# Second LayerNorm transposed by DMA, a third slot for the pair sums, and a new plan for the order on TensorE

## Chip, cores, metric

One core of a Trainium2 chip. The metric is the device time of one execution in microseconds; medians of several runs, compared within the same rounds on the same chip. The kernel before was timed anew with each of the four sets of runs: medians 1119.2 to 1120.4, so times from different sets compare to about 1 us.

## The reference

A transformer block over 2048 tokens of width 1024: LayerNorm, attention with 32 heads of 32, residual, LayerNorm, a feed-forward part of width 3584 with tanh-GELU, residual. Inputs and output are bf16.

```
h  = x + softmax(q k^T * 32**-0.5) v @ wo        # q, k, v from layernorm(x) @ wqkv
h2 = h + gelu(layernorm(h) @ w1 + b1) @ w2 + b2
```

## The kernel before

The kernel first lists all its work as tasks, each with an engine, an assumed duration and its dependencies. A list scheduler then plays these tasks through on assumed clocks and writes down the order on each engine. That order is fixed in the program, and on the chip an engine stands where its next instruction still lacks an input: ScalarE stood 18.6 us ahead of the exps in the kernel before, 10.5 of them for scores. So a constant such as the assumed length of an exp changes nothing that is computed, but it changes the order.

```
def schedule(self, pick_pe, switch=0.1, ...):     # assumed cost of a change of array mode on TensorE
    ...
                    if e == E.PE:
                        if state["mode"] != t.mode:
                            start += switch
MM = 0.2140                                       # assumed: 512 columns
def c_act(n, ap_bias=False):                      # assumed: ScalarE; 0.943 us for an exp of 1024
    return 0.090 + (0.093 if ap_bias else 0.0) + n / 1200.0
...
NPS = 2                                           # slots for pair sums
NFI = 2                                           # buffers of the finish
```

Attention runs in 512 rounds (64 jobs of eight). A round is eight score matmuls (row tiles: the array is split by rows, and four heads run at once: eight matmuls of 273 ns each lie within 0.40 us in the prediction's timeline), two exps on ScalarE, one pair sum on VectorE (it adds the two halves of the exps, for the row sums of the softmax), eight value matmuls and four row-sum matmuls (column tiles: the array is split by columns). Six PSUM banks hold scores, three slots of which a round uses two; the other banks serve a job's output and one or two groups of background work.

```
for q in range(2):
    act(... a.activation(PT[:, s, 2*q:2*q+2, :], psum[:, 2*u:2*u+2, :], ACT.Exp, ...), 1024, kind="exp")
z = unit["ps"] % NPS
dve(... v.tensor_tensor(PS[:, z, :, :], PT[:, s, :, 0:256], PT[:, s, :, 256:512], ALU.add), ...)
```

The background work is projections, the output projection, FFN1 (full array) and FFN2 (column tiles). Tokens go in eight chunks of 256. At the turn of a chunk the second LayerNorm makes two tiles, one after the other through one buffer, and transposes them for FFN1:

```
def ln2_tile(R, c, t, evac):
    o, bo = R.xb.next()                           # one buffer for both tiles
    layer_norm([(hch[:, c % 2, t, :], ..., o, bo)], LN2_PRIO)
    if evac == "dma":
        dma_t(hnT[:, t, :, :], o, [bo], [B_hnT[t]], prio=-1)
    else:                                         # eight TensorE transposes and a VectorE copy
        transposes(group(f"t{c}.{t}"), o, bo, hnT[:, t, :, :], B_hnT[t], evac)
...
PLAN = [F2[0], 2, F2[1], 5, F2[2], 5, F2[3], 2]   # FFN2 groups of the older chunk, FFN1 blocks between
for c in range(2, NC):
    if c > 2:
        wo(R1, c - 1)
    ln2(R1, c - 1, "dve")
    mixed(R1, c - 1, c - 2, PLAN)
    attention(c)
```

The softmax here doesn't subtract the row's maximum and nothing guards it: scores larger than these inputs give would overflow.

Of the kernel before, what the change touches and what calls it, by code (L numbers as in the profile page):

```python
# [7 lines left out]
ACT = mybir.ActivationFunctionType  # L8
ALU = mybir.AluOpType
# [3 lines left out]
P = 128  # L13
BF = dt.bfloat16
F32 = dt.float32
# [48 lines left out]
class Graph:  # L64
# [44 lines left out]
        return t  # L109


    def schedule(self, pick_pe, switch=0.1, dma_rate=260.0, dma_lat=2.0, fetch=4.7):
        for i, t in enumerate(self.tasks):
            t.left = len(t.deps)
            for d in t.deps:
# [10 lines left out]
        n = 0  # L126
# [11 lines left out]
        while n < total:  # L138
# [5 lines left out]
            for e in self.ENGS:  # L144
                while free[e] <= now + 1e-9:
# [6 lines left out]
                    if e == E.PE:  # L152
                        t = pick_pe(rd, now, state, up)
                    else:
                        t = min(rd, key=lambda x: (x.prio, num[x]))
                        if up and t.prio > 0:

                            for (rt, _, u) in up[:6]:
                                if u.prio < t.prio and rt < now + 0.6 * t.occ:
                                    t = None  # L160
# [5 lines left out]
                    if e == E.PE:  # L166
# [3 lines left out]
                        i = state["pe"] // 256  # L170
# [142 lines left out]
def build_kernel(nc, A_x, A_wqkv, A_wo, B_w1, B_b1, B_w2, B_b2, out):  # L313
# [9 lines left out]
    SCALE = DH ** -0.5  # L323
# [25 lines left out]
    def sb(area, name, shape, dtype, split=1, parts=1):  # L349
        off, n = area.take(shape, dtype)  # L350
        h = nc.alloc_sbuf_tensor_at(name, shape, dtype, offset=off)
        step = n // split
        bufs = []
        for i in range(split):
            ps = [gr.buf("SB", off + i * step, off + (i + 1) * step, (name, i)) for _ in range(parts)]
            bufs.append(ps if parts > 1 else ps[0])
        return h, (bufs if split > 1 else bufs[0])

    top = Area(BASE)
# [25 lines left out]
    NPT = 7  # L385
    PT, B_PT_ = sb(top, "PT", [P, NPT, 4, 512], BF, 2 * NPT)
    B_PT = [B_PT_[2 * s:2 * s + 2] for s in range(NPT)]
    NPS = 2
    PS, B_PS = sb(top, "PS", [P, NPS, 4, 256], BF, NPS)
    NFI = 2  # L390
    OS, B_OS = sb(top, "OS", [P, NFI, 256], F32, NFI)
    DT, B_DT = sb(top, "DT", [P, NFI, 256], F32, NFI)
    RT, B_RT = DT, B_DT
    RB, B_RB = sb(top, "RB", [P, NFI, 8], F32, NFI)
    pt_hi = top.cur
    junk = PT[:, NPT - 1, 0:2, :]
    B_junk = B_PT[NPT - 1][0]
    NOT = 2
    F2 = [(0, 0), (0, 1), (1, 0), (1, 1)]
    OT, B_OT_ = sb(top, "OT", [P, NOT, G, 256], BF, NOT * G)  # L400
# [30 lines left out]
    R1 = Set()  # L431
# [20 lines left out]
    psum = nc.alloc_psum_tensor("ps", [P, 8, 512], F32)  # L452
# [3 lines left out]
    qd = nc.dram_tensor("q_scratch", [G, 3, P, 512], BF, kind="Internal").ap()  # L456
    B_qd = [[gr.buf() for _ in range(3)] for _ in range(G)]

    MM = 0.2140

    def c_dve_ps(n):
        return (120 + n) / 960.0 + 0.02

    def c_dve(n, x=1):
        return (62 + n / x) / 960.0 + 0.02

    def c_act(n, ap_bias=False):
        return 0.090 + (0.093 if ap_bias else 0.0) + n / 1200.0

    def pe(fns, occ, reads=(), writes=(), kind="bg", mode="full", prio=0, after=()):  # L470
        return gr.add(E.PE, fns, occ, 0.16, reads, writes, prio, kind, mode, after)
# [15 lines left out]
    def mm(g, lhsT, rhs, start, stop, reads, cols=(0, 512)):  # L487
        c0, c1 = cols
        occ = MM * (c1 - c0) / 512.0 + 0.0015
        fns = []  # L490
# [13 lines left out]
    def act(fn, n, reads=(), writes=(), prio=0, ap_bias=False, kind=""):  # L504
        return gr.add(E.Activation, fn, c_act(n, ap_bias), 0.14, reads, writes, prio, kind)

    def dve(fn, occ, reads=(), writes=(), prio=0, after=()):
        return gr.add(E.DVE, fn, occ, 0.08, reads, writes, prio, after=after)
# [157 lines left out]
    class Job:  # L666
# [10 lines left out]
        def round(self):  # L677
            r, g = self.r, self.g
            self.r += 1
            us = []  # L680
            for _ in range(2):
                us.append(unit["n"] % unit["of"])
                unit["n"] += 1
            s = unit["pt"] % NPT
            unit["pt"] += 1
            fns = []
            for i in range(2):
                for hh in range(4):
                    r0 = 32 * hh
                    fns.append(lambda p, i=i, hh=hh, r0=r0: p.matmul(  # L690
                        psum[:, 2 * us[hh // 2] + hh % 2, 256 * i:256 * i + 256],
                        KT[r0:r0 + 32, g, 256 * r + P * i:256 * r + P * i + P], QT[r0:r0 + 32, self.slot, :],
                        start=True, stop=True, tile_position=(r0, 0)))
            pe(fns, 0.217, reads=[B_KT[g][r], B_QT[self.slot]], writes=[B_ps[2 * u + k] for u in us for k in range(2)],
               kind="qk", mode="row")
            for q in range(2):
                u = us[q]
                act(lambda a, u=u, q=q: a.activation(PT[:, s, 2 * q:2 * q + 2, :], psum[:, 2 * u:2 * u + 2, :], ACT.Exp, bias=0.0, scale=SCALE),  # L698
                    1024, reads=[B_ps[2 * u], B_ps[2 * u + 1]], writes=[B_PT[s][q]], kind="exp")
            direct = self.direct or (self.final and r == 7)  # L700
            if not direct:
                z = unit["ps"] % NPS
                unit["ps"] += 1
                dve(lambda v: v.tensor_tensor(PS[:, z, :, :], PT[:, s, :, 0:256], PT[:, s, :, 256:512], ALU.add), c_dve(1024, 2),  # L704
                    reads=B_PT[s], writes=[B_PS[z]], prio=-1)
            fns = []
            for i in range(2):
                for hh in range(4):
                    fns.append(lambda p, i=i, hh=hh: p.matmul(  # L709
                        psum[32 * hh:32 * hh + 32, self.bank, 0:256], V[:, g, 2 * r + i, 32 * hh:32 * hh + 32],  # L710
                        PT[:, s, hh, 256 * i:256 * i + 256], start=r == 0 and i == 0, stop=r == 7 and i == 1,
                        tile_position=(0, 32 * hh), skip_group_check=True))
            t = pe(fns, 0.217, reads=B_PT[s] + [B_V[g][r]], writes=[self.buf], kind="pv", mode="col")
            pvs.append(t)
            job_of[t] = self
            self.dens.append((r, s if direct else z, direct))
            if len(self.dens) == 2:
                self.den(*self.dens.pop(0))
            if r == 7:
                self.den(*self.dens.pop(0))  # L720
                self.finish()
# [11 lines left out]
        def finish(self):  # L733
            g, c = self.g, self.c
            f = unit["fi"] % NFI
            unit["fi"] += 1
            dve(lambda v: v.transpose(DT[:, f, :], psum[:, self.bank, 256:512]), c_dve_ps(256),  # L737
                reads=[self.buf], writes=[B_DT[f]], prio=-1)
            if not self.final:
                dve(lambda v: v.tensor_copy(OS[:, f, :], psum[:, self.bank, 0:256]), c_dve_ps(256),  # L740
                    reads=[self.buf], writes=[B_OS[f]], prio=-1)
            dve(lambda v: v.reciprocal(RB[:, f, :], DT[:, f, :].rearrange("p (b j) -> p b j", j=32)[:, :, 0]), 0.15,
                reads=[B_DT[f]], writes=[B_RB[f]])
            dve(lambda v: v.transpose(RT[:, f, :], RB[:, f, :].unsqueeze(2).broadcast_to((P, 8, 32))), c_dve(256),
                reads=[B_RB[f]], writes=[B_RT[f]])
            dve(lambda v: v.tensor_tensor(OT[:, c % NOT, g, :], psum[:, self.bank, 0:256] if self.final else OS[:, f, :], RT[:, f, :], ALU.mult),
                c_dve_ps(256), reads=[self.buf if self.final else B_OS[f], B_RT[f]], writes=[B_OT[c % NOT][g]])

    def wblock(R, src_ap):
# [27 lines left out]
    def wo(R, c):  # L777
        for j in range(2):
            ws = wo_w(R, j)
            for t in range(2):  # L780
                wo_group(R, c, j, t, ws)

    def ln2_tile(R, c, t, evac):
        o, bo = R.xb.next()
        layer_norm([(hch[:, c % 2, t, :], B_hch[c % 2][2 * t:2 * t + 2], o, bo)], LN2_PRIO)
        if evac == "dma":
            dma_t(hnT[:, t, :, :], o, [bo], [B_hnT[t]], prio=-1)
        else:
            transposes(group(f"t{c}.{t}"), o, bo, hnT[:, t, :, :], B_hnT[t], evac)

    def ln2(R, c, evac):
        for t in range(2):
            ln2_tile(R, c, t, evac)
# [70 lines left out]
    def mixed(R, c1, c2, plan):  # L864
        blk = 0
        for p in plan:
            if isinstance(p, int):
                ffn1(R, c1, range(blk, blk + p))
                blk += p
            else:  # L870
                ffn2(R, c2, *p)
# [89 lines left out]

    b1_on_partitions()
    wo(R1, 0)
    ln2(R1, 0, "dve")
    for h in range(3):
        for g in range(G):
            spill_q(g, h)
# [3 lines left out]
    def attention(c):  # L971
        for g in range(G):
            attend(g, c)
            c2, g2 = divmod(G * c + g + NQ, G)
            if c2 < NC:
                load_q(g2, c2)
# [4 lines left out]
    for c in range(2, NC):  # L981
        if c > 2:
            wo(R1, c - 1)
        ln2(R1, c - 1, "dve")
        mixed(R1, c - 1, c - 2, PLAN)
        attention(c)
    L = NC - 1
# [195 lines left out]
```

## Time and profile before

| | before |
|---|---|
| time, median of 4 | 1120.39 us |
| first exp starts, last exp ends | 15.9, 1052.4 us |
| after the last exp | 65.6 us |
| TensorE, ScalarE busy | 96%, 93% |
| changes of array mode on TensorE | 1213 |

Most lines are in the prediction. Two more of the page: the chain of work that ended last, by engine, and the exps' group (busy time and mean length; idle time before them).

```profile
PE 81%; ACT 11%; DVE 6%; issue 1%; POOL 0%; DVEq 0%; POOLq 0%
...
L698 ACT ACTIVATE PT<-ps 128x1024 bf16<-128x1024 f32 x1024 | 966.6, 1034 | 18.6 <-PE ps L690 10.5
```

The chain that sets the end runs over TensorE for 81% of the time. ScalarE shows little idle time, but the exps' busy time of 966.6 us is longer than they need (1024 x 0.9125 = 934 us by their starts), so some 33 us of it, by these two numbers, is waiting inside records.

### The profile page before, as it was taken

The page shows a single profiled execution, that of the slowest core. Times are in us where ns is not written, and L with a number is a line of the kernel's source. Part 1 is how long each engine was busy: PE and PEld are TensorE (multiplying, and loading weights), DVE is VectorE, ACT ScalarE, POOL GpSimd, SP SyncE. Part 2 cuts the span into 40 slices and gives each one's busy share as a digit, 9 for nine tenths or more (in the row PEclk, how much of TensorE's full clock was granted, in tenths as well). Part 3 has the DMA queues.
Part 4 walks back from the last instruction along what each step waited for, and adds up shares of the span by engine and source line. Part 5 has one row for each costly group of instructions (what it writes and reads, how often), then busy time and mean ns, then how long its engine had stood idle before and what let it go on. Part 6 is the DMA issues. An engine that isn't in the chain of part 4 may idle for free.

```text
span 1118.0 us, 44121 instructions
## 1 busy us (share of the span) xinstructions
PE 1072.1 (96%) x20225; PEld 594.9 (53%) x20229; DVE 825.6 (74%) x1475; ACT 1042.5 (93%) x1135; POOL 19.2 (2%) x37
## 2 busy tenths in 40 slices
PE   8999999999999989999999999999989999999999
PEld 6646464644445635554554555456535544564485
DVE  7465756676767987887788788868878776787663
ACT  5889999999999999999999999999999999999661
POOL 1000000000000000000000000000000000000000
PEclk9999999999999999999999999999999999999999
DMA  6960100012236526484747548455837368697570
GB/s 191 197 162 4 40 4 3 4 55 87 83 97 174 165 73 204 122 258 141 217 143 225 176 126 251 134 176 162 259 95 230 97 199 244 212 264 225 165 244 20
DMA packets 248390, 165.66 MB, mean 148 GB/s; under 512 B 35979, under 2 KB 246027, under 8 KB 248204
## 3 DMA queue, kind: packets, MB, share of 16 engines
q1 hardware_dynamic: 248204, 162.83, 49.8%
q8 instruction: 159, 2.61, 1.0%
q14 instruction: 27, 0.22, 0.1%
HBM read 152.31 MB, written 7.34 MB: 143 GB/s over the span
## 4 chain that ended last, share of the span: by engine, by line
PE 81%; ACT 11%; DVE 6%; issue 1%; POOL 0%; DVEq 0%; POOLq 0%
PE ps L497 31%; PE ps L500 23%; PE ps L690 12%; ACT PT L698 11%; PE ps L709 9%; PE ps L728 5%; DVE PS L704 2%; PE ps L888 1%; DVE gT L814 1%; PE ps L580 1%; DVE stg L593 0%; DVE a_os L859 0%; DVE gT L833 0%; ACT a_th L832 0%; DVE a_sq L830 0%
## 5 line engine op out<-in xcount | busy, mean ns | idle before, releaser
L698 ACT ACTIVATE PT<-ps 128x1024 bf16<-128x1024 f32 x1024 | 966.6, 1034 | 18.6 <-PE ps L690 10.5
L704 DVE TENSOR_TENSOR PS<-PT 128x1024 bf16<-128x1024 bf16 x495 | 328.1, 683 | 78.5 <-PE ps L728 42.5
L500 PE MATMUL ps<-hnT,w1r 128*128 128x256 bf16 x1632 | 206.7, 273 | 8.0 <-DVE gT L814 5.6
L690 PE MATMUL ps<-QT,KT 32*128 32x256 bf16 x4096 | 204.0, 273 | 9.3 <-ACT PT L698 8.2
L497 PE MATMUL ps<-w2r,gT 128*32 128x512 bf16 x3056 | 210.3, 382 | 1.4 <-DVE gT L833 1.2
L709 PE MATMUL ps<-PT,V 128*32 128x256 bf16 x4096 | 184.9, 274 | 6.0 <-ACT PT L698 4.6
L500 PEld LDWEIGHTS ps<-hnT,w1r 128*128 128x128 bf16 x1632 | 146.9, 98 | 60.7 <-issue 38.2
L690 PEld LDWEIGHTS ps<-QT,KT 32*128 32x128 bf16 x4096 | 60.8, 92 | 162.3 <-ACT PT L698 99.4
L728 PE MATMUL ps<-PS,ones 128*32 128x256 bf16 x1980 | 139.0, 276 | 2.2 <-DVE PS L704 1.7
L497 PE MATMUL ps<-xnT,Wall 128*32 128x512 bf16 x1888 | 128.2, 381 | 4.3 <-DVE stg L593 2.8
L709 PEld LDWEIGHTS ps<-PT,V 128*32 128x32 bf16 x4096 | 96.4, 96 | 58.4 <-issue 17.3
L497 PEld LDWEIGHTS ps<-w2r,gT 128*32 128x32 bf16 x3056 | 71.6, 96 | 67.2 <-issue 25.1
L814 DVE TENSOR_TENSOR gT<-ps,b1f 128x512 bf16<-128x512 f32 x98 | 67.3, 687 | 32.5 <-PE ps L500 31.4
L728 PEld LDWEIGHTS ps<-PS,ones 128*32 128x32 bf16 x1980 | 51.4, 95 | 42.9 <-DVE PS L704 22.6
L833 DVE SCALAR_TENSOR_TENSOR gT<-a_th,gT 128x1024 bf16<-128x1024 f32 x49 | 59.7, 1219 | 14.6 <-ACT a_th L832 14.4
L497 PEld LDWEIGHTS ps<-xnT,Wall 128*32 128x32 bf16 x1888 | 44.2, 96 | 46.8 <-issue 13.2
L497 PE MATMUL ps<-w1r,OT 128*32 128x512 bf16 x896 | 61.4, 381 | 2.0 <-DVE hch L774 1.4
L830 DVE SCALAR_TENSOR_TENSOR a_sq<-a_sq,gT 128x1024 bf16<-128x1024 bf16 x49 | 59.8, 1221 | 0.9
L497 PE MATMUL ps<-Wall,xnT 128*32 128x256 bf16 x1536 | 52.4, 274 | 1.8 <-DVE V L593 0.9
L832 ACT ACTIVATE a_th<-a_sq 128x1024 f32<-128x1024 bf16 x49 | 51.8, 1058 | 0.2
L737 DVE STREAM_TRANSPOSE DT<-ps 128x256 f32<-128x256 f32 x64 | 28.6, 446 | 24.5 <-PE ps L728 24.5
L497 PEld LDWEIGHTS ps<-Wall,xnT 128*32 128x32 bf16 x1536 | 37.9, 96 | 11.4 <-issue 7.7
(86 smaller groups left out, 630.5 us busy)
## 6 DMA issues: line engine op xcount, KB each, us to landing
w2r<-in_B_w_dram SPq DMA_DIRECT2D x105, 512.0 KB, 5.7
w1r<-in_B_w_dram SPq DMA_DIRECT2D x102, 512.0 KB, 4.7
w1r<-in_A_wo_dram SPq DMA_DIRECT2D x28, 512.0 KB, 4.1
wk<-in_B_w_dram SPq DMA_DIRECT2D x9, 512.0 KB, 6.1
xrb<-in_A_x_dram SPq DMA_DIRECT2D x16, 256.0 KB, 4.2
Wall<-in_A_wqkv_dram SPq DMA_DIRECT2D x16, 256.0 KB, 5.3
wv<-in_B_w_dram SPq DMA_DIRECT2D x8, 512.0 KB, 7.7
a_x<-in_A_x_dram SPq DMA_DIRECT2D x28, 128.0 KB, 3.9
```

Of the source, the lines that this page charges most:

```text
L497: fns.append(lambda p, j=j: p.matmul(dst(32 * j, 32 * j + 32), lhsT[:, 32 * j:32 * j + 32], rhs, start=start, stop=stop, tile_position=(0, ...
L500: t.alt = [lambda p: p.matmul(dst(0, P), lhsT, rhs, start=start, stop=stop, skip_group_check=True)]
L690: fns.append(lambda p, i=i, hh=hh, r0=r0: p.matmul(psum[:, 2 * us[hh // 2] + hh % 2, 256 * i:256 * i + 256], KT[r0:r0 + 32, g, 256 * r + P ...
L698: act(lambda a, u=u, q=q: a.activation(PT[:, s, 2 * q:2 * q + 2, :], psum[:, 2 * u:2 * u + 2, :], ACT.Exp, bias=0.0, scale=SCALE), 1024, r ...
L704: dve(lambda v: v.tensor_tensor(PS[:, z, :, :], PT[:, s, :, 0:256], PT[:, s, :, 256:512], ALU.add), c_dve(1024, 2), reads=B_PT[s], writes= ...
L709: fns.append(lambda p, i=i, hh=hh: p.matmul(psum[32 * hh:32 * hh + 32, self.bank, 0:256], V[:, g, 2 * r + i, 32 * hh:32 * hh + 32], PT[:, ...
L728: fns.append(lambda p, i=i, hh=hh, src=src: p.matmul(psum[32 * hh:32 * hh + 32, self.bank, 256:512], ones32[:, :], src[:, hh, :], start=False,
L737: dve(lambda v: v.transpose(DT[:, f, :], psum[:, self.bank, 256:512]), c_dve_ps(256), reads=[self.buf], writes=[B_DT[f]], prio=-1)
L814: gate[c] = dve(lambda v, xh=xh, fc=fc, grp=grp: v.tensor_tensor(xh, psum[:, grp.bank, :].rearrange("p (f n) -> p f n", f=2), b1f[:, fc:fc ...
L830: dve(lambda v: v.scalar_tensor_tensor(v4(sq), v4(sq), C2, xh, ALU.add, ALU.mult), c_dve(n), reads=[b_sq] + b_xh, writes=[b_sq], prio=1)
L832: act(lambda a: a.activation(th, sq, ACT.Tanh, bias=0.0, scale=K2 / 2), n, reads=[b_sq], writes=[b_th], prio=-1, kind="tanh")
L833: t = dve(lambda v: v.scalar_tensor_tensor(xh, v4(th), 1.0, xh, ALU.add, ALU.mult), c_dve(n), reads=[b_th] + b_xh, writes=b_xh, prio=1)
```

## The change

Its intent: take the second LayerNorm's transposes off TensorE and VectorE, use one finish buffer instead of two so that a third pair-sum slot fits, and plan the order with constants nearer to the chip. Call the parts D (transposes by DMA), S (slot), P (planner's constants).

The diff is cut to its main lines:

```diff
-    def schedule(self, pick_pe, switch=0.1, dma_rate=260.0, dma_lat=2.0, fetch=4.7):
+    def schedule(self, pick_pe, switch=0.108, dma_rate=260.0, dma_lat=2.0, fetch=4.7):
-    NPS = 2
+    NPS = 3
-    NFI = 2
+    NFI = 1
     ... (OS, DT, RB become separate tensors, indexed [f][:] instead of [:, f, :])
-    MM = 0.2140
+    MM = 0.2150
-        return 0.090 + (0.093 if ap_bias else 0.0) + n / 1200.0
+        return 0.072 + (0.093 if ap_bias else 0.0) + n / 1200.0
+    EXP = (0.930, 0.915)
-                act(lambda a, u=u, q=q: ... ACT.Exp ..., kind="exp")
+                t = act(lambda a, u=u, q=q: ... ACT.Exp ..., kind="exp")
+                t.occ = EXP[q]
-    ln2(R1, 0, "dve")
+    ln2(R1, 0, "dma")
-        ln2(R1, c - 1, "dve")
+        ln2(R1, c - 1, "dma")
```

More of the change, by code (lines that the diff above doesn't have):

```diff
@@ L387, in build_kernel @@
     B_PT = [B_PT_[2 * s:2 * s + 2] for s in range(NPT)]
-    NPS = 2
+    NPS = 3
     PS, B_PS = sb(top, "PS", [P, NPS, 4, 256], BF, NPS)
-    NFI = 2
-    OS, B_OS = sb(top, "OS", [P, NFI, 256], F32, NFI)
-    DT, B_DT = sb(top, "DT", [P, NFI, 256], F32, NFI)
+    NFI = 1
+    OS, DT, RB, B_OS, B_DT, B_RB = [], [], [], [], [], []
+    for i in range(NFI):
+        for h, b, nm, n in ((OS, B_OS, "OS", 256), (DT, B_DT, "DT", 256), (RB, B_RB, "RB", 8)):
+            x, y = sb(top, f"{nm}{i}", [P, n], F32)
+            h.append(x)
+            b.append(y)
     RT, B_RT = DT, B_DT
-    RB, B_RB = sb(top, "RB", [P, NFI, 8], F32, NFI)
     pt_hi = top.cur
@@ L697, in round @@
                 u = us[q]
-                act(lambda a, u=u, q=q: a.activation(PT[:, s, 2 * q:2 * q + 2, :], psum[:, 2 * u:2 * u + 2, :], ACT.Exp, bias=0.0, scale=SCALE),
+                t = act(lambda a, u=u, q=q: a.activation(PT[:, s, 2 * q:2 * q + 2, :], psum[:, 2 * u:2 * u + 2, :], ACT.Exp, bias=0.0, scale=SCALE),
                     1024, reads=[B_ps[2 * u], B_ps[2 * u + 1]], writes=[B_PT[s][q]], kind="exp")
+                t.occ = EXP[q]
             direct = self.direct or (self.final and r == 7)
@@ L736, in finish @@
             unit["fi"] += 1
-            dve(lambda v: v.transpose(DT[:, f, :], psum[:, self.bank, 256:512]), c_dve_ps(256),
+            dve(lambda v: v.transpose(DT[f][:], psum[:, self.bank, 256:512]), c_dve_ps(256),
                 reads=[self.buf], writes=[B_DT[f]], prio=-1)
             if not self.final:
-                dve(lambda v: v.tensor_copy(OS[:, f, :], psum[:, self.bank, 0:256]), c_dve_ps(256),
+                dve(lambda v: v.tensor_copy(OS[f][:], psum[:, self.bank, 0:256]), c_dve_ps(256),
                     reads=[self.buf], writes=[B_OS[f]], prio=-1)
-            dve(lambda v: v.reciprocal(RB[:, f, :], DT[:, f, :].rearrange("p (b j) -> p b j", j=32)[:, :, 0]), 0.15,
+            dve(lambda v: v.reciprocal(RB[f][:], DT[f][:].rearrange("p (b j) -> p b j", j=32)[:, :, 0]), 0.15,
                 reads=[B_DT[f]], writes=[B_RB[f]])
-            dve(lambda v: v.transpose(RT[:, f, :], RB[:, f, :].unsqueeze(2).broadcast_to((P, 8, 32))), c_dve(256),
+            dve(lambda v: v.transpose(RT[f][:], RB[f][:].unsqueeze(2).broadcast_to((P, 8, 32))), c_dve(256),
                 reads=[B_RB[f]], writes=[B_RT[f]])
-            dve(lambda v: v.tensor_tensor(OT[:, c % NOT, g, :], psum[:, self.bank, 0:256] if self.final else OS[:, f, :], RT[:, f, :], ALU.mult),
+            dve(lambda v: v.tensor_tensor(OT[:, c % NOT, g, :], psum[:, self.bank, 0:256] if self.final else OS[f][:], RT[f][:], ALU.mult),
                 c_dve_ps(256), reads=[self.buf if self.final else B_OS[f], B_RT[f]], writes=[B_OT[c % NOT][g]])
```

## The prediction

> **What bounds the kernel now.** I read first the page's busy line and the slices, then the costliest groups, then busy time by stretches of 20 us, then the waits, then single stretches of the timeline. The busy line:
>
> ```profile
> PE 1072.1 (96%) x20225; PEld 594.9 (53%) x20229; DVE 825.6 (74%) x1475; ACT 1042.5 (93%) x1135; POOL 19.2 (2%) x37
> ```
>
> Two engines are nearly full, TensorE and ScalarE, and VectorE has room. Busy records stretch where work overlaps or waits, so I went to starts in the trace. Exps (line L698) that follow one another without a wait start 0.904 and 0.921 us apart in turn, mean 0.9125. There are 1024 of them, so 934 us; the other ScalarE work between the first exp (15.9 us) and the end of the last (1052.4 us) is 49 tanh at 0.93 us and 12 us of copies in the lead: together 992 us in a stage of 1036.5 us. TensorE's work in the same stage is close to that too. Its cost per piece is the distance from start to start: 0.217 us for four column tiles of 512 columns, 0.110 for 256 columns, 0.056 for a transpose, and about 0.104 us more wherever the array changes between row tiles (scores), column tiles (most of the rest) and the full array (FFN1 and transposes). In the timeline this last cost looks so:
>
> ```profile
> 153.63 0.83 PE L497 MATMUL ps<-Wall,xnT 128*32 128x256 bf16 x24
> ...
> 154.40 0.40 PE L690 MATMUL ps<-QT,KT 32*128 32x256 bf16 x8
> ...
> 154.72 0.51 PE L497 MATMUL ps<-Wall,xnT 128*32 128x256 bf16 x12
> ```
>
> The columns are start, length, engine, line and count. The 24 are six packs of four, 6 x 0.110 = 0.66, yet scores start 0.77 after them: 0.11 for the change. The eight scores are two packs, 0.22, and the next work starts 0.32 after them: 0.10 again. The instruction order of this kernel has 1213 such changes, so 126 us of TensorE's time. With these costs the whole TensorE program adds up to 1053 us: 11 before the first score, 977 between the first and last score, 65 after the last.
>
> So between first and last exp ScalarE has 992 us of work and TensorE 977 us, in 1036 us. Neither is the only bound: scores can run ahead by little more than one exp (three score buffers, two used per round), so a round with too much TensorE work makes ScalarE wait, and one with too little leaves TensorE waiting. The stretches show both cases and the tail:
>
> ```profile
> 400.00:420.00 20.00, 15.79 (x292) 6.97 (x296) 16.61 (x24) 19.45 (x21) 0.00 (x0) 0.89 0.07 19
> 440.00:460.00 20.00, 20.00 (x330) 11.79 (x328) 16.24 (x28) 19.63 (x21) 0.00 (x0) 1.00 0.79 229
> 820.00:840.00 20.00, 16.82 (x340) 8.43 (x336) 14.15 (x30) 19.86 (x23) 0.99 (x1) 1.00 0.48 144
> 1080.00:1100.00 20.00, 19.95 (x144) 13.86 (x143) 15.67 (x16) 10.79 (x19) 0.00 (x0) 1.00 0.14 45
> ```
>
> (busy PE, PE loads, DVE, ACT, POOL, then clock, DMA share, GB/s). At 400 and 820 us TensorE has run out of background work and waits for ScalarE; at 440 it is full; after 1060 it alone sets the end.
>
> [...]This kernel transposes 12 tiles of the first LayerNorm[...]: 3.6 us to landing against 4.2 us for a plain load of the same 256 KB.
>
> ```profile
> xrb<-in_A_x_dram SPq DMA_DIRECT2D x16, 256.0 KB, 4.2
> ...
> xnT<-xb SPq DMA_TRANSPOSE x12, 3.6
> ```
>
> [...]eight in one DMA land here in 3.2 to 4.7 us[...].
>
> **The change part by part.** (1) The second LayerNorm's transposes. Seven chunks of two tiles lose eight TensorE transposes and one VectorE copy each:
>
> ```profile
> L580 PE MATMUL ps<-ident,xb 128*128 128x128 bf16 x144 | 13.6, 224 | 1.4 <-DVE a_os L859 1.3
> L586 DVE COPY hnT<-ps 128x1024 bf16<-128x1024 bf16 x14 | 9.5, 681 | 0.3 <-PE ps L580 0.3
> ```
>
> Of the 144, 32 belong to the lead and stay; 112 go: 112 x 0.056 = 6.3 us of TensorE. VectorE loses 14 copies, 9.5 us, which is worth little by itself. Fourteen DMA transposes come in, 1.33 us of issuing each on a queue with room and 256 KB each beside 163 MB of traffic.
>
> (2) The order on TensorE is planned anew. Counted in both instruction orders, the changes of array mode fall from 1213 to 1171: 42 x 0.104 = 4.4 us. Most of these are visits to the full array that the transposes made. Together TensorE falls from 1053.0 to 1042.3 us, 10.7 less. But eight column packs of FFN2 move behind the last score, so the tail rises from 64.6 to 66.3 us, 1.7 more, and the stage between first and last score falls by 12.4, from 977.4 to 965.0. The planner's exps go from 0.943 to a mean of 0.9225 us, nearer to the measured 0.9125, its mode change from 0.100 to 0.108, its 512 columns from 0.2140 to 0.2150: all nearer to the trace. Exps themselves are no faster.
>
> (3) The pair sums' third slot. Their waits in the present kernel:
>
> ```profile
> DVE PS L704 <- PE ps L728: 42.5, 69, 5.7
> PEld ps L728 <- DVE PS L704: 22.6, 84, 0.8
> ```
>
> The first, VectorE waiting for a slot, costs nothing by itself, as VectorE has room. The second, TensorE's weight loads waiting for a pair sum, is partly hidden: matmuls run on meanwhile. I give the slot 3 us. The single finish buffers cost nothing that I can see: the finish is a chain on VectorE alone, 64 times in 1000 us, and its instructions are in order anyway.
>
> How much of the 12.4 us becomes time? ScalarE's 992 us do not shrink. I took both instruction orders, cut them into rounds, and summed for groups of rounds the larger of TensorE's and ScalarE's work, with the costs above. In groups of two rounds this gives 1036.9 before and 1026.3 after; in groups of four 1017.0 and 1012.0. The first happens to equal the measured stage of 1036.5, so I lean on it: 10.6 less, with 5 less as the cautious value. In the new order the thin stretch near 400 us is filled: 16 rounds from round 192 hold 33.9 us of TensorE work where they held 26.4. Sum: 1120.6 - 10.6 + 1.7 - 3 = 1108.7, say 1109 us.
>
> **The rivals.** First, the DMA's landing takes the place of the transpose's wait. There is one buffer for the normalised tile, so VectorE may write the second tile only when the first tile's DMA has landed. In the new order VectorE has in five chunks only 11 to 14 instructions between the two writes, 4.7 to 5.9 us of work by the durations in the groups; issue to landing is 3.2 to 4.7 us in the lead from the start of the issue. It just fits, but plain loads in this stage take longer:
>
> ```profile
> w2r<-in_B_w_dram SPq DMA_DIRECT2D x105, 512.0 KB, 5.7
> w1r<-in_B_w_dram SPq DMA_DIRECT2D x102, 512.0 KB, 4.7
> ```
>
> If a transpose queued behind them took 8 us, VectorE, which is in order, would stand 3 us in seven chunks, TensorE's row sums would wait for pair sums, and up to 20 us would be lost: then 1115 to 1125. Against it: the third slot, and a plan that counts on some 4.5 us. I give this, in a form that eats most of the gain, 15%.
>
> Second, ScalarE's floor: if the present waits of ScalarE come from latency and not from overfull rounds, less TensorE work helps little. Then only the thin stretches and part of the mode changes count, 3 to 6 us: 1115 to 1118. For it: ScalarE is at 19.7 to 20.0 of 20 in most stretches. Against it: exps start 0.954 us apart on average against 0.9125 without waits, so 42 us of delay lie there. 25%.
>
> Third, the better plan wins more than the counted work: misplanned waits of TensorE, some 80 us over the whole span by the costs above, fall by a quarter. Then 1090 to 1100. 12%; the floor from ScalarE's work, 16 + 992 + 66 = 1074, leaves room.
>
> **Range and chances.** The middle is 1109; the weak cases end near 1117, the good one near 1099. Faster by over 2% means below 1098.2, which needs the third case nearly whole: 0.11. Slower by over 2%, above 1143, needs DMA stalls far beyond those of the lead: 0.01. Within 2%: 0.88.
>
> **What would show it.** The transposes and copies of this stage gone and TensorE's busy time some 10 us less; last exp ending near 1040 instead of 1052; the tail near 66 to 68 us. Right on the slot: the wait of VectorE for L728 well under 42 us and the weight loads' wait on pair sums under 22. Right on the DMA: landing of the new transposes under 5.5 us, and VectorE's write of the tile waiting for them only a few us in all; over 15 us there would be the first rival. An unchanged gap between exps (0.954 us on average) would be the second. The prediction is wrong if the time is under 1099, above all if TensorE's waits fell by more than 20 us, or if it is over 1117.

## The result and the profile after

The changed kernel takes 1111.07 us (1108.92 to 1112.25, four runs) against 1120.39: ratio 0.991, 95% interval 0.9886 to 0.9934. A ratio here is the mean time of one kernel's runs over that of the other's of the same rounds, so it is not quite the ratio of the medians.

| | before | after | predicted |
|---|---|---|---|
| time | 1120.39 | 1111.07 | 1109 |
| first exp to last exp | 1036.5 | 1026.4 | 10.6 less, and 3 more for the slot |
| after the last exp | 65.6 | 66.5 | 1.7 more |

The page of the changed kernel, busy line, chain by engine and exps' group:

```profile
PE 1063.2 (96%) x20093; PEld 592.1 (53%) x20093; DVE 819.0 (74%) x1461; ACT 1025.6 (92%) x1135; POOL 19.0 (2%) x37
...
ACT 52%; PE 45%; DVE 2%; issue 1%; POOL 0%; DVEq 0%; POOLq 0%
...
L703 ACT ACTIVATE PT<-ps 128x1024 bf16<-128x1024 f32 x1024 | 953.5, 1083 | 23.4 <-PE ps L715 12.9
```

TensorE's busy time is 8.9 us less and half of the chain now lies on ScalarE. The starts of exps that follow one another lie 0.935 us apart on average where it was 0.954. The stretches that the prediction showed, now (same columns):

```profile
400.00:420.00 20.00, 15.97 (x297) 6.28 (x295) 14.47 (x21) 16.85 (x19) 0.00 (x0) 1.00 0.82 219
420.00:440.00 20.00, 19.50 (x327) 12.30 (x328) 16.35 (x27) 15.93 (x18) 0.00 (x0) 0.91 0.48 141
440.00:460.00 20.00, 19.95 (x369) 11.06 (x368) 16.26 (x26) 19.95 (x22) 0.00 (x0) 1.00 0.40 114
820.00:840.00 20.00, 18.80 (x396) 8.62 (x396) 14.85 (x38) 19.58 (x23) 1.10 (x2) 1.00 0.87 216
1080.00:1100.00 20.00, 19.96 (x105) 9.96 (x104) 8.61 (x9) 4.68 (x8) 0.00 (x0) 1.00 0.04 14
```

The busy column of ScalarE tells little here, since its records hold waits (1.083 us for an exp in the mean, where 0.9125 is enough from start to start): it was as full before. The starts tell more. From 440 us to the end of the last exp, exps at 0.9125 us and tanh at 0.93 leave 23.1 us unused before and 8.7 after (summed over the starts in both traces). The thin stretch at 820 is nearly filled, the one at 400 is not: there ScalarE now stands as well. The timeline of the changed kernel shows how (VectorE's other instructions and the DMA queue left out):

```profile
414.91 1.22 DVE L839 SCALAR_TENSOR_TENSOR gT<-a_th,gT 128x1024 bf16<-128x1024 f32 x1 [1.51 <-ACT a_th L838]
...
416.19 1.91 PE L502 MATMUL ps<-w2r,gT 128*32 128x512 bf16 x32 [1.79 <-DVE gT L839]
...
420.40 3.06 PE L502 MATMUL ps<-w2r,gT 128*32 128x512 bf16 x32 [2.30 <-DVE gT L839]
...
423.23 1.08 PE L715 MATMUL ps<-PT,V 128*32 128x256 bf16 x16
...
423.93 1.94 ACT L703 ACTIVATE PT<-ps 128x1024 bf16<-128x1024 f32 x2 [4.84 <-PE ps L715]
```

In TensorE's fixed order 64 FFN2 matmuls stand ahead of the value matmuls (L715). They wait for GELU on VectorE (1.79 and 2.30 us), the value matmuls stand behind them, and the exps wait 4.84 us for those. The 16 value matmuls also take 1.08 us at half the clock (0.50 granted from 423.23 to 424.31 us), where 0.62 is seen at full clock (at 434.29 us). The order has this queue built in: the planner's own times have the same standstill (1.94 and 2.31 us of TensorE). The lines' numbers have moved by 5 or 6 with the change: scores L690 are L695, exps L698 are L703, value products L709 are L715, row sums L728 are L734.

What became of the removed work and of the new waits, in the changed kernel's groups and waits:

```profile
L585 PE MATMUL ps<-ident,xb 128*128 128x128 bf16 x32 | 2.3, 219 | 0.0
...
L578 DVE TENSOR_SCALAR xb<-hch,mvr,rden 128x1024 bf16<-128x1024 bf16 x14 | 7.6, 542 | 1.0 <-DMA hnT<-xb 0.9
...
DVE PS L710 <- PE ps L734: 28.8, 29, 4.0
...
PEld ps L734 <- DVE PS L710: 10.9, 45, 0.5
```

The 112 transposes are gone. VectorE waits 0.9 us in all for a transpose to land, although the landings are longer than in the same kernel's lead (3.2 to 4.9 us, median 3.4), by the view of the tile that they write:

```profile
DMA to landing us min/median/max: 3.1/4.9/7.7
```

The waits around the pair sums have fallen, by a third (42.5 to 28.8) and by half (22.6 to 10.9), as the slot was to do.

### The profile page after: what moved, and what is told of

Read it like the earlier page. It is cut to its first block, busy times and chain, and to the rows that moved or that the text cites. A ratio compares the mean times of both kernels' runs of the same rounds, so it can differ in the third digit from the quotient of the medians.

```text
span 1109.7 us, 43839 instructions
## 1 busy us (share of the span) xinstructions
PE 1063.2 (96%) x20093; PEld 592.1 (53%) x20093; DVE 819.0 (74%) x1461; ACT 1025.6 (92%) x1135; POOL 19.0 (2%) x37
## 4 chain that ended last, share of the span: by engine, by line
ACT 52%; PE 45%; DVE 2%; issue 1%; POOL 0%; DVEq 0%; POOLq 0%
ACT PT L703 49%; PE ps L502 16%; PE ps L505 14%; PE ps L695 6%; PE ps L715 5%; ACT a_th L838 3%; PE ps L734 2%; PE ps L894 1%; DVE PS L710 1%; DVE gT L839 0%; DVE hch L780 0%; DVE a_sq L836 0%; PE ps L585 0%; ACT xnT L588 0%; ACT V L596 0%
## 5 line engine op out<-in xcount | busy, mean ns | idle before, releaser
L703 ACT ACTIVATE PT<-ps 128x1024 bf16<-128x1024 f32 x1024 | 953.5, 1083 | 23.4 <-PE ps L715 12.9
L710 DVE TENSOR_TENSOR PS<-PT 128x1024 bf16<-128x1024 bf16 x495 | 332.4, 685 | 109.1 <-ACT PT L703 76.2
L695 PE MATMUL ps<-QT,KT 32*128 32x256 bf16 x4096 | 203.8, 273 | 15.0 <-ACT PT L703 13.6
L502 PE MATMUL ps<-w2r,gT 128*32 128x512 bf16 x3024 | 204.1, 382 | 4.5 <-DVE gT L839 4.4
L715 PE MATMUL ps<-PT,V 128*32 128x256 bf16 x4096 | 183.5, 275 | 4.2 <-ACT PT L703 3.2
L695 PEld LDWEIGHTS ps<-QT,KT 32*128 32x128 bf16 x4096 | 61.1, 92 | 174.9 <-ACT PT L703 140.2
L734 PE MATMUL ps<-PS,ones 128*32 128x256 bf16 x1980 | 137.8, 275 | 0.5 <-DVE PS L710 0.4
L715 PEld LDWEIGHTS ps<-PT,V 128*32 128x32 bf16 x4096 | 94.6, 96 | 61.5 <-issue 22.6
L734 PEld LDWEIGHTS ps<-PS,ones 128*32 128x32 bf16 x1980 | 52.2, 96 | 23.9 <-DVE PS L710 10.9
L838 ACT ACTIVATE a_th<-a_sq 128x1024 f32<-128x1024 bf16 x49 | 55.0, 1123 | 2.3 <-DVE a_sq L836 2.2
L743 DVE STREAM_TRANSPOSE DT<-ps 128x256 f32<-128x256 f32 x64 | 28.5, 446 | 17.4 <-PE ps L734 17.1
```

What stands on the lines that cost most here:

```text
L502: fns.append(lambda p, j=j: p.matmul(dst(32 * j, 32 * j + 32), lhsT[:, 32 * j:32 * j + 32], rhs, start=start, stop=stop, tile_position=(0, ...
L695: fns.append(lambda p, i=i, hh=hh, r0=r0: p.matmul(psum[:, 2 * us[hh // 2] + hh % 2, 256 * i:256 * i + 256], KT[r0:r0 + 32, g, 256 * r + P ...
L703: t = act(lambda a, u=u, q=q: a.activation(PT[:, s, 2 * q:2 * q + 2, :], psum[:, 2 * u:2 * u + 2, :], ACT.Exp, bias=0.0, scale=SCALE), 102 ...
L710: dve(lambda v: v.tensor_tensor(PS[:, z, :, :], PT[:, s, :, 0:256], PT[:, s, :, 256:512], ALU.add), c_dve(1024, 2), reads=B_PT[s], writes= ...
L715: fns.append(lambda p, i=i, hh=hh: p.matmul(psum[32 * hh:32 * hh + 32, self.bank, 0:256], V[:, g, 2 * r + i, 32 * hh:32 * hh + 32], PT[:, ...
L734: fns.append(lambda p, i=i, hh=hh, src=src: p.matmul(psum[32 * hh:32 * hh + 32, self.bank, 256:512], ones32[:, :], src[:, hh, :], start=False,
```

## Experiments

Three theories. **W**, the prediction's idea in its shortest form: the time is TensorE's work in the planned order (durations as in the prediction) plus a constant of about 66 us, 65 before and 67 after. The prediction's own sum, by rounds, is taken up further below. **P**: the order itself counts, how well it spreads background work over the rounds, and the constants made it better. **D**: the landing of the transposes costs, and eats what they save. The planner's end, quoted below, is the time at which the kernel's scheduler on its assumed clocks expects its last instruction to end: a by-product of the build.

Half-clock stretches also turned out to matter: the trace's clock record shows TensorE granted 0.5 of its clock for multiples of 3.4 us. I put the cost of such a stretch at half its length if TensorE is wanted, as matmuls take twice as long in it (0.22 us instead of 0.11 in no_plan, below).

| kernel | TensorE work | planner's end | half-clock after the lead began, length / 2 | span in the profile | time, median |
|---|---|---|---|---|---|
| before | 1052.9 | 1115.2 | 3.4 | 1118.0 | 1120.39 |
| D S P (the change) | 1042.2 | 1108.4 | 3.4 | 1109.7 | 1111.07 |
| only_dma (D) | 1044.4 | 1121.4 | 13.6 | 1133.1 | 1136.21 |
| only_slot (S) | 1051.7 | 1123.8 | 11.9 | 1131.4 | 1133.83 |
| only_plan (P) | 1054.4 | 1118.7 | 1.7 | 1118.9 | 1119.5 |
| no_plan (D S) | 1041.8 | 1126.4 | 27.2 | 1144.8 | 1141.41 |
| no_dma (S P) | 1054.8 | 1113.5 | 1.7 | 1113.1 | 1114.64 |
| no_slot (D P) | 1045.0 | 1110.4 | 0 | 1107.0 | 1110.67 |

Every kernel's output was correct.

### only_dma

```diff
 (before)
-    ln2(R1, 0, "dve")
+    ln2(R1, 0, "dma")
-        ln2(R1, c - 1, "dve")
+        ln2(R1, c - 1, "dma")
```

> The old planner constants, two slots for pair sums, double finish buffers, and only the second LayerNorm's transposes moved to the DMA. Theory W (the end is TensorE's work plus a constant 66 us of waits): its instruction order holds 1044.4 us of TensorE work against 1052.9 before and 1042.2 in the changed kernel, so about 1111 us. Rival P (what counts is how the planned order balances exps and background work, and the constants did it): the kernel's own planner ends at 1121.4 where it gave 1115.2 for before, so about 1126 us, slower than before. Rival D (the landing of the transposes stalls VectorE): over 1120 with more than 15 us of VectorE waiting for a transpose to land.

Measured 1136.21 us, ratio 1.0151 (1.0132 to 1.0171): slower than before by 16 us, though it has 8.5 us less TensorE work. W falls. P and D have the direction, and the size is 10 us beyond P. VectorE waited only 0.4 us for a landing, so D in the form of a VectorE wait falls too. VectorE and TensorE together waited 0.9 us for landings. Where the time is, see no_plan.

### only_plan

```diff
 (before)  switch=0.1 -> 0.108, MM 0.2140 -> 0.2150, c_act 0.090 -> 0.072, exps at EXP = (0.930, 0.915)
```

> Only the planner's constants changed (mode switch, matmul, ScalarE, exps). W: the order holds 1054.4 us of TensorE work, so about 1121 us, as before. P: if the constants made the gain, 1110 to 1114; by the planner's own end (1118.7 against 1115.2 of before) about 1122, with the last exp near 1034 and a tail of over 80 us, as 86 us of TensorE work stand behind the last score.

Measured 1119.5 us, ratio 0.9995 (0.997 to 1.0021): nothing by itself. But the shape is quite different. Its stretches, with the usual columns:

```profile
500.00:600.00 100.00, 98.33 (x1800) 52.77 (x1796) 82.33 (x141) 100.00 (x110) 1.11 (x2) 1.00 0.60 179
...
1050.00:1150.00 100.00, 66.31 (x445) 43.10 (x443) 26.89 (x30) 18.43 (x35) 0.00 (x0) 1.00 0.34 111
```

ScalarE is full (100.00 of 100), the last exp ends at 1032.5, 20 us earlier than before, and then TensorE alone works off 86 us that were left over. The faster attention phase was worth nothing here, as background work stayed behind. Both W and P by the planner's end foresaw this one; P's other number, 1110 to 1114 if the constants alone made the gain, falls.

### no_slot

```diff
 (the changed kernel)
-    NPS = 3
+    NPS = 2
-    NFI = 1                     (and the finish buffers as before)
+    NFI = 2
```

> The changed kernel with two slots for pair sums and double finish buffers, as before. W: 1045.0 us of TensorE work against 1042.2, so about 1114 us. If the third slot is worth the 3 us that the prediction gave it, 1114 as well, but then the weight loads' wait on pair sums rises from 10.9 to over 20 us. P: planner's end 1110.4 against 1108.4, so about 1113. A time within 1 us of 1111 says the slot gives nothing.

Measured 1110.67 us, ratio 0.9922 (0.9903 to 0.9942), against 1111.07 with the slot: no worth of the slot is seen. The two ratios to before, 0.9922 and 0.991, differ by 0.001 and are uncertain by 0.003 together, so the 3 us of the prediction are not ruled out by the times alone. The slot's waits are back, by the view of the waits:

```profile
DVE PS L707 <- PE ps L731: 35.9, 52, 3.9
...
PEld ps L731 <- DVE PS L707: 25.3, 97, 0.5
```

25.3 us of weight loads waiting for pair sums instead of 10.9, and no loss of time seen, which fits waits that lie beside running matmuls (the row-sum matmuls themselves waited 0.8 us in all for pair sums). This is also a different order (last exp at 1027.5, tail 79.6), so a small worth of the slot could be masked by it.

### no_plan

```diff
 (the changed kernel)
-    switch=0.108, MM = 0.2150, 0.072, EXP = (0.930, 0.915)
+    switch=0.1,   MM = 0.2140, 0.090, no EXP
```

> The changed kernel with the old planner constants (transposes by DMA and third slot kept). W: 1041.8 us of TensorE work, so about 1108 us, not slower than the changed kernel. P: the planner's own end is 1126.4 with its slow exps, so 1120 to 1130, and the last exp ends after 1050 us.

Measured 1141.41 us, ratio 1.02 (1.0162 to 1.0238), slower even than P's range. Its four runs spread from 1136.93 to 1146.58, and the profile is of the slowest. The order with the least TensorE work of these eight is the slowest; W is dead as a rule. Here one sees where the time goes, in 10 us stretches at the last chunk's turn:

```profile
955.00:965.00 10.00, 7.14 (x140) 2.71 (x140) 7.81 (x23) 10.00 (x13) 1.10 (x2) 0.91 0.64 143
965.00:975.00 10.00, 8.33 (x92) 3.46 (x93) 5.65 (x12) 9.50 (x11) 0.00 (x0) 0.50 0.58 139
```

and in the timeline there:

```profile
966.86 0.55 DVE L578 TENSOR_SCALAR xb<-hch,mvr,rden 128x1024 bf16<-128x1024 bf16 x1 [0.99 <-DMA hnT<-xb]
...
967.48 1.24 SPq L529 DMA_TRANSPOSE hnT<-xb  x1
...
971.82 0.39 PE L505 MATMUL ps<-hnT,w1r 128*128 128x256 bf16 x1
...
972.69 3.17 PE L505 MATMUL ps<-hnT,w1r 128*128 128x256 bf16 x14
```

The second tile waits for the first one's landing, is transposed, and FFN1 starts at 971.8. From 958.8 us until then TensorE has only attention to do (no matmul of FFN2 stands there; the kernel before runs them all through its turn), and the granted clock is 0.50 over the whole ten microseconds. When FFN1 comes, 14 matmuls take 3.17 us, 0.22 each, where 0.11 is usual. The busy column does not show this (8.33 of 10): slow matmuls are long records.

I measured this turn in all kernels: from VectorE's write of the first tile to FFN1's first matmul, the share of the array's capacity used (columns streamed at full clock, times the part of the array in use). Chunk turns at about 510, 610, 710, 820 and 950 us:

| kernel | used share in the five turns |
|---|---|
| before | 0.76, 0.75, 0.76, 0.62, 0.79 |
| only_dma | 0.87, 0.81, 0.82, 0.66, 0.30 |
| no_plan | 0.76, 0.44, 0.54, 0.82, 0.30 |
| the change | 0.86, 0.70, 0.86, 0.81, 0.84 |
| order_dma2 (below) | 0.85, 0.85, 0.85, 0.85, 0.84 |

The turns last 12 to 25 us. Against a share of 0.82, the three thin turns of no_plan (13.7, 12.5 and 12.2 us long) lost 13.7 x 0.38 + 12.5 x 0.28 + 12.2 x 0.52 = 15 us of TensorE. So D exists, but as a hole in TensorE's background work at the turn and only in small part as a wait of VectorE (5.1 us for landings in all of no_plan); and it appears where the order has no FFN2 work left to lie there. Half-clock stretches follow thin work: over all kernels here 32 began between 15 us and the tail's end, and in the 3.4 us before each the used share was 0.17 to 0.375. The converse holds nearly as well if the traces are cut into the 3.413 us steps in which the clock record changes: of 4449 such steps at full clock in the 14 kernels, these 32 were followed by half clock, and of the other 4417 only five had used 0.375 or less (the least 0.31, at 1020 us in the kernel before). TensorE was not idle before these stretches: it was busy for 23 to 70% of the 3.4 us before each. In the kernel before the two stretches, at 402 and 419 us, came after used shares of 0.34 and 0.22; in the changed one, at 28 and 421 us, after 0.375 and 0.25. What sets the granted clock was not shown.

### only_slot

```diff
 (before)  NPS = 2 -> 3, NFI = 2 -> 1
```

> Only the third slot for pair sums and the single finish buffers; transposes on TensorE, old constants. W (TensorE's work plus some 66 us, plus what half-clock stretches cost): 1051.7 us of work, so about 1118 us, at most 2 us from before. P (the order as planned): the planner's end is 1123.8 against 1115.2 of before, so 1126 to 1130. If the slot has a worth of its own, under 1117.

Measured 1133.83 us, ratio 1.0138 (1.0119 to 1.0158): slower than before, 4 us beyond P's range, with 11.9 us of half-clock loss. A buffer more, with nothing else, made the kernel 1.4% slower, through the order that the planner made with it. Its chunk turns are not thin (0.68 to 0.82); its half-clock stretches after the lead lie at 420 and 1024 to 1080. By the starts, ScalarE leaves 11.1 us unused after 1000 us where the kernel before leaves 1.6; at 1024 us FFN2 matmuls wait 2.39 us for GELU, the standstill of 414 us again. Why the planner made that order I did not find out.

### no_dma

```diff
 (the changed kernel)
-    ln2(..., "dma")
+    ln2(..., "dve")
```

> The changed kernel with the transposes put back on TensorE and VectorE (new constants and third slot kept). W: 1054.8 us of TensorE work, 12.6 more than the changed kernel, so about 1121 us, as before, with the last exp near 1034 and a tail near 86 us. P: planner's end 1113.5 against 1108.4, so 1114 to 1116.

Measured 1114.64 us, ratio 0.9959 (0.9939 to 0.998). P's number, not W's. With 1054.8 us of TensorE work, more than before, and 1232 changes of mode, more than before, it is still 0.4% faster than before.

### exps_only and rest_only

Which of the constants? Both are the kernel before with D and two slots.

```diff
 exps_only:  c_act 0.090 -> 0.072, EXP = (0.930, 0.915); switch and MM as before
 rest_only:  switch 0.1 -> 0.108, MM 0.2140 -> 0.2150; exps at 0.943 as before
```

> The kernel before with transposes by DMA and only the ScalarE constants of the change (0.090 to 0.072, exps at 0.930 and 0.915); mode switch 0.100, matmul 0.2140 and two slots stay. P with the exps' length as what counts: planner's end 1100.3, so 1101 to 1106, against 1136 with all constants old. If the mode switch's length is what counts, it stays over 1120. W: 1044.3 + 66 = 1110.

Measured 1109.44 us, ratio 0.9895 (0.9876 to 0.9914).

> The same with only the other two constants: mode switch 0.108 and matmul 0.2150, exps left at 0.943. P: planner's end 1118.0, [...]half-clock stretches come on top: 1122 to 1135, and the last exp after 1050. If the longer mode switch is what counts, under 1115. W: 1043.9 + 66 = 1110.

Measured 1122.72 us, ratio 1.0009 (0.9983 to 1.0036), last exp at 1055.9, one half-clock stretch after the lead, of 17.1 us at 959. P's range, 1122 to 1135, holds.

ScalarE's assumed lengths are what makes D pay (the exps' above all: the same edit takes 18 ns off the few tanh and copies): with them alone D goes from 1136.21 to 1109.44; the other two constants alone bring it to 1122.72, near the time of before. They help by half as much, but make no gain. P's range for exps_only was 3 us too low, and W's 1110 fits it; W misses rest_only by 13 us. In exps_only the turns are used to 0.80 to 0.87, in rest_only two of five only to 0.56 and 0.49. The starts in the traces separate the kernels by this constant, whatever else they have. From 440 us to the last exp, ScalarE leaves 23 to 45 us unused in the five kernels planned with exps of 0.943 us (before, only_dma, only_slot, no_plan, rest_only) and 6 to 11 in the nine planned with 0.930 and 0.915. A reading that fits, but which I only argue: a planner that believes in exps of 0.943 us where they take 0.9125 sees more room for TensorE in each round than there is, puts more background work into it, and has none left at the turn.

The parts depend on each other. The constants are worth nothing alone (only_plan), but 19 us with the slot (1133.83 against 1114.64), 26 with the DMA (1136.21 against 1110.67) and 30 with both. With them, D gains 9 us without the slot (1119.5 against 1110.67) and 4 with it (1114.64 against 1111.07). One rival is untested: the knobs of the kernel before (PLAN, AHEAD) may have been picked for its own order, and then any part alone would upset that order.

### switch_107 and switch_109

How much is chance? The changed kernel with the assumed mode switch moved by 1 ns.

```diff
-    switch=0.108
+    switch=0.107     (and 0.109)
```

> The changed kernel with one constant moved by 1 ns, mode switch 0.107 instead of 0.108: nothing that runs is different but the order. P: planner's end 1105.1 against 1108.4, so about 1107 to 1109. If the result of 1111 follows from the work taken off TensorE, it is within 1 us of 1111 (1042.0 us of work against 1042.2).

Measured 1108.19 us, ratio 0.9889 (0.987 to 0.9907), as P said.

> The same with 0.109. P: planner's end 1113.8, so 1113 to 1117, several us slower than the changed kernel for 1 ns in one constant. W: 1042.9 us of work, so 1111 to 1112.

Measured 1117.38 us, ratio 0.9967 (0.9952 to 0.9983), 0.4 us over P's range.

So 1 ns more in a constant takes away two thirds of the gain, and the planner foresaw the direction of both. The changed kernel's 0.9% is one draw from a spread of about that size.

### order_dma2 and order_pe3

If the order is what counts, search it: combinations of the planner's lookahead, the backlog of value products at which it opens a new job, the places of the FFN2 groups, two or three slots, transposes by DMA or not, all with the new constants, ranked by the planner's end.

```diff
 (the changed kernel)
 order_dma2: NPS = 2, NFI = 2; AHEAD 0.3 -> 1.1; PLAN = [F2[0], F2[1], 7, F2[2], 5, F2[3], 2]
 order_pe3:  ln2 "dve"; AHEAD 0.3 -> 0.8; PV_START 5 -> 6; PLAN = [F2[0], 1, F2[1], 5, F2[2], 5, F2[3], 3]
```

> An order searched for with the kernel's own planner: transposes by DMA, new constants, two slots; lookahead 1.1 us instead of 0.3, both first FFN2 groups ahead of FFN1. Planner's end 1099.9, TensorE work 1044.9[...]. P: about 1101 us, below the changed kernel's 1111. W: 1044.9 + 66 = 1111, no gain over the changed kernel. No half-clock stretch after the lead is expected.

Measured 1101.06 us (1099.67 to 1101.62), ratio 0.9841 (0.9827 to 0.9855). The one half-clock stretch lies at 27 us, in the lead.

> The same search without the DMA: transposes on TensorE, new constants, three slots; lookahead 0.8 us, five waiting value products become six, FFN2 groups one block earlier. Planner's end 1100.5, TensorE work 1049.5. If the transposes by DMA are what makes the gain, this is no faster than 1115. P: about 1102 us, so the DMA would not be needed at all. W: 1049.5 + 66 = 1115.

Measured 1101.79 us (1100.88 to 1104.26), ratio 0.9852 (0.9835 to 0.987).

Both beat both kernels, by 10 us the changed one, and both agree with P within 1 us. The second has the transposes still on TensorE: the DMA is not needed for the gain. W is out by 10 and 13 us. The stretches of order_dma2:

```profile
400.00:500.00 100.00, 97.26 (x1776) 52.12 (x1772) 84.73 (x136) 97.24 (x106) 0.55 (x1) 1.00 0.61 183
500.00:1000.00 500.00, 488.17 (x9052) 263.96 (x9040) 401.82 (x694) 499.82 (x543) 6.07 (x9) 1.00 0.69 196
```

and of the changed kernel:

```profile
400.00:500.00 100.00, 95.22 (x1682) 51.42 (x1684) 82.07 (x128) 92.72 (x102) 0.00 (x0) 0.98 0.62 183
500.00:1000.00 500.00, 483.31 (x9034) 263.07 (x9027) 399.45 (x695) 498.72 (x542) 6.82 (x10) 1.00 0.67 193
```

The stall at 414 us is gone (ScalarE 97.24 of 100 instead of 92.72), and between 500 and 1000 us, where ScalarE is full in both, order_dma2 has 488 us of TensorE's busy time instead of 483; by columns streamed the gain there is 3 us (406 against 403 us of the whole array at full clock). Its last exp ends at 1032.1 and its tail is 65.9: an early end of the exps and a short tail at once, which none of the eight of the table has.

For the eight kernels with all the new constants (the change, no_slot, only_plan, no_dma, switch_107, switch_109, order_dma2, order_pe3) the span in the profile lies between 3.4 us under and 1.7 over the planner's end. For exps_only it lies 8 us over, and for those with old exps 3 to 18, most where the half-clock loss is largest; the planner knows of no clock.

## Why the prediction was right or wrong

- **The number.** 1109 was said, 1111.07 measured, inside 1099 to 1117, and within 2% as said.
- **TensorE's removed work**, 10.7 us: borne out as an amount, 8.9 us less busy time, the transposes gone and 1171 changes of mode.
- **The stage shrinks by 10.6 us, the tail grows by 1.7.** Measured 10.1 and 0.9, though with the slot's 3 us the stage was to shrink by 13.6 and the last exp to end near 1040; it ended at 1043.2. The size was nearly right; as a rule it fails. With old exps the same D has less TensorE work than before and is 1.5% slower (only_dma); without D, an order is as fast as the best (order_pe3). The sum over two rounds, redone with such costs for the plans of all 14 kernels (1038.6 and 1023.3 us for before and after, where the prediction had 1036.9 and 1026.3), plus the tail, comes within 7 us of the measured difference to before in the nine kernels planned with the shorter exps, but is 16 to 36 us too fast in the four others with the old length. It counts work, and sees neither a hole with no work to put in nor the halved clock after it (0.50 from 965 to 975 us in no_plan).
- **"The thin stretch near 400 us is filled."** The work was there, but of the 33.9 us in 16 rounds four rounds hold 11.2, and they wait for GELU: ScalarE stands 4.84 us at 419 us.
- **"All nearer to the trace. Exps themselves are no faster."** This step failed. The prediction gave the constants no worth but a share of the 4.4 us of mode changes. The runs give ScalarE's constants 27 us where D is in (1136.21 against 1109.44), all constants 19 us where only the slot is in, and nothing where neither is (only_plan); and no_dma is faster than before with 19 mode changes more. So that the total came out near is partly luck: 1 ns in the mode switch's constant gave 1108 or 1117.
- **The slot, 3 us.** Not seen: its waits fell as said (42.5 to 28.8, 22.6 to 10.9), the time did not (no_slot, 1110.67), but the runs resolve no better than 3 us, and the order differs too. It was the one term of the sum without a counted path to the end. The sum without it is 1111.7.
- **First rival, the landing.** Landing was to stay under 5.5 us: the median was 4.9, the longest 7.7, and VectorE waited 0.9 us. The rival does live in other orders, at 15 us in no_plan, but mostly as a hole in TensorE's work and a halved clock; VectorE stood for 5.1 us.
- **Second rival, ScalarE's floor.** Not in the form given: the gap between exps fell from 0.954 to 0.935 us. From 440 us on ScalarE leaves only 8.7 us unused, though, so little further gain lies there (order_dma2 leaves 6.1); more lies in the 11.5 us between 60 and 300 us (7.5 in order_dma2) and the 7.7 between 400 and 440 (3.1).
- **Third rival, a better plan.** It was given 12% and had the right idea: TensorE's waits did not fall in the changed kernel (span less counted work is 65.1 us before and 67.5 after, by the table), so it was not realised there; but order_dma2, with 53.1, shows 10 us more to be had that way.

## What to carry to other kernels

When the instruction order is fixed by a planner, a change of work is also a change of order, and the two must be told apart: test parts in all combinations, move a constant by a hair to see the spread, and only then give the gain to a part. Calibrate the planner's durations from start-to-start distances in the trace first; when they were right here, the planner's own end came within 3.4 us of the span in all eight kernels, and a search over its knobs was worth more than the change. A long transfer in place of a short engine step (a landing of 4.9 us here, for eight transposes of 0.056 and a copy of 0.68) can leave a hole: in the changed kernel the busiest engine had work at the last turn (used share 0.84), in no_plan it had little (0.30), and the granted clock was 0.50 from 965 to 975 us. Look for holes there, and at the granted clock right after them.
